# Attention ahead of two MoE layers: the 1e-9 of the softmax sums is added on ScalarE behind the last exponential, and the periodic order is placed anew

## The chip, the core and the metric

The kernel runs on one core of a Trainium2 chip. The core has TensorE (PE, matrix products and transposes), VectorE (DVE), ScalarE (ACT), GpSimd (POOL) and SyncE (SP, which issues the DMAs here). Each has its own queue and does its instructions in order; semaphores hold an instruction until what it reads or overwrites is ready. The metric is the device time of one execution in microseconds.

## The reference

Attention over 4 batches, 12 heads, 448 positions and 64 dimensions, with RMS-normalized q and k; its result goes, as 1792 rows of 768, through two MoE-like layers.

```python
q_n, k_n = (rmsnorm(q, g_q), rmsnorm(k, g_k))
scores = scale * np.matmul(q_n, k_n.transpose(0, 1, 3, 2))
scores = scores - np.max(scores, axis=-1, keepdims=True)
attn = np.exp(scores)
attn = attn / (np.sum(attn, axis=-1, keepdims=True) + 1e-09)
x = np.matmul(attn, v)                   # then to (batch * seq, heads * dim)
h = x @ moe_w_in;   x = (h / (1 + np.exp(-h))) @ moe_w_out
h = x @ moe2_w_in;  out = np.maximum(h, 0) ** 2 @ moe2_w_out
```

## The kernel before

**Attention** goes by pairs of heads: 4 batches of 6 pairs, 24 pairs. `prepare` loads q and k (qk), squares them, sums the squares (ms), makes the inverse root with a logarithm, an exponential and Newton steps (L641, L645, L649 to L664), multiplies (n, L672), transposes on TensorE (L684) and splits the result into an upper and a lower part (T; q_hi on ScalarE at L693 and L695, q_lo on VectorE at L700 and L702). `weigh` takes the 448 rows in three blocks of 128 for both heads and one block that mixes the last 64 rows of both (Q, Em). For each block TensorE makes the scores (L750, L757), VectorE the negated row maximum (mx, L772), ScalarE the exponential (E, L780), which also writes the sum of each row into one of the 7 columns of the tile `sum`. TensorE transposes E (L793), and ScalarE and VectorE copy the result from PSUM to SBUF (PTa and PTb, L563 and L565).

`attend` inverts the sums: on VectorE an add of 1e-9 (L823) and a reciprocal (L824), both in place on 128 x 7; TensorE transposes them (L820), VectorE copies them out (inv, L833), and SP stores them to DRAM and reads them back spread over the partitions (rd, R, L840 and L848). TensorE multiplies with v (L859), ScalarE copies that (xf), and GpSimd multiplies it by R (L879). The result is stored to DRAM (keep_x); of the first two batches it is also split into an upper part on ScalarE (x_hi, L575) and a lower part on GpSimd (x_lo, L584). Squares, Newton steps, the product n and Q run on GpSimd too, but for the first pairs.

**The MoE layers** follow on all 1792 rows, with every weight split into an upper and a lower part by ScalarE, VectorE and GpSimd.

**What sets the order.** A planner in the kernel (`Plan`) issues the steps. For attention it follows a table: step kind n of pair i stands at PERIOD x i plus its entry in LOADS or TABLE, plus a correction in FIRST for the first eight pairs; `plan.fix` ties a step to that place and to one engine. These numbers only sort the steps; on the chip each engine runs its queue as the semaphores allow. Steps without a place, all of the MoE layers among them, are put in by the planner by its own costs, and so move when the table moves.

The add and the reciprocal before, and their places:

```python
        def invert(e):
            nc.vector.tensor_scalar(sums.ap, sums.ap, 1e-9, None, ALU.add)
            nc.vector.reciprocal(sums.ap, sums.ap)
        step("invert", at, {"dve": (0.33, None, False)}, invert, writes=keys)
```

Of the kernel before, what the change touches and what calls it, by code (L numbers as in the profile page):

```python
# [9 lines left out]
F32 = mybir.dt.float32  # L10
# [3 lines left out]
AF = mybir.ActivationFunctionType  # L14
# [3 lines left out]
P = 128  # L18
# [20 lines left out]
PERIOD = 8.685  # L39
# [7 lines left out]
    "load_g": [1.36], "gains": [9.92], "warm": [-40.0],  # L47
    "load_qk": [-28.94, -23.71],
    "load_v": [1.94],
    "store_r": [22.9],  # L50
    "spread": [32.29, 33.29, 32.79],
    "keep_x": [54.22],
}
TABLE = {
    "squares": [-21.02, -18.06],
    "sums": [-7.69, -7.64],
    "log": [-3.92],
    "root": [-3.53],
    "newton": [-3.8, -2.59, -2.29, -1.99, -0.73],
    "norm": [1.57, 0.55],  # L60
    "turn_q": [6.83, 5.67],
    "q_hi": [8.48, 6.66],
    "q_lo": [9.18, 7.52],
    "scores": [13.72, 12.32, 13.07],
    "row_max": [15.15, 17.35, 13.28, 14.08, 14.62, 15.69, 16.81],
    "exp": [16.55, 18.85, 13.99, 14.74, 15.93, 17.6, 18.23],
    "turn_e": [19.76, 20.0, 19.13, 19.52, 20.23, 20.78, 20.47],
    "e_copy": [20.45, 20.59, 19.97, 19.97, 21.23, 21.23, 20.93, 22.3],
    "mask": [11.37],
    "mixed": [14.9],  # L70
    "attend": [24.63, 26.52],
    "invert": [19.61],
    "turn_s": [20.71],
    "inverse": [22.51],
    "pv_copy": [28.18],
    "attended": [38.49],
    "x_hi": [47.8],
    "x_lo": [74.71],
}
# [337 lines left out]
def kernel(  # L417
# [136 lines left out]

# [255 lines left out]
    def attend(i, vr, PT, sums, last):  # L810
# [938 lines left out]
```

## Time and profile before

| | us |
|---|---|
| median of 3 runs (lowest, highest) | 1142.46 (1142.25, 1143.43) |
| the profiled execution, its own time | 1144.96 |
| its span, first to last instruction | 1143.1 |
| busy in the span: PE, DVE | 1113.3, 945.9 |
| busy in the span: ACT, POOL | 609.4, 284.3 |

The span is cut into stretches below: two inside attention, its end, and the MoE layers. A share of busy time over the whole span says little, since TensorE fills the MoE layers and VectorE is the fullest engine of attention; the rows by stretch, the chain of work that ended last, and the timelines of single engines have to be read together. A matmul's row can be longer than the distance to the next one, since matmuls are pipelined; the same holds in a small way for ScalarE and VectorE. "Granted clock" is TensorE's, 1.00 for 2.4 GHz.

### The profile page before, as it was taken

How to read it: one execution, taken by the hardware profiler on the slowest of the kernel's cores; microseconds unless marked ns; L12 is line 12 of the kernel's file. 1: busy time of each engine (PE TensorE's matmuls, PEld its weight loads, DVE VectorE, ACT ScalarE, POOL GpSimd, SP SyncE). 2: the span in 40 equal slices, each digit the busy share in tenths (PEclk: the TensorE clock that was granted, in tenths of full speed). 3: DMA queues.
4: the chain of work that ended last, by engine and by line, in shares of the span. 5: the costliest groups of instructions: out<-in, count | busy, mean ns of one | idle time of the engine just before them, and what ended most of it. 6: DMA issues, size and time to landing. Idle time of an engine off the chain costs nothing.

```text
span 1143.1 us, 20235 instructions
## 1 busy us (share of the span) xinstructions
PE 1113.3 (97%) x7463; PEld 1000.7 (88%) x7463; DVE 945.9 (83%) x1660; ACT 609.4 (53%) x1273; POOL 284.3 (25%) x364
## 2 busy tenths in 40 slices
PE   8999999999999999999999999999999999999998
PEld 6776667779999898999999988999999999999997
DVE  7999999968687879887778798687888976888886
ACT  7988889965563547455554343544224435333321
POOL 5777788420101002100010010001230201122220
PEclk8999999999999999999999999999999999999999
DMA  7343344258646566677677579878758794555454
GB/s 185 99 123 121 109 122 125 84 177 275 210 148 219 161 207 216 224 251 250 221 264 228 196 232 360 290 277 318 276 194 300 239 330 180 180 192 181 168 171 132
DMA packets 122435, 235.29 MB, mean 206 GB/s; under 512 B 12216, under 2 KB 86112, under 8 KB 122336
## 3 DMA queue, kind: packets, MB, share of 16 engines
q1 hardware_dynamic: 122096, 233.80, 61.2%
q8 instruction: 59, 0.97, 0.3%
q14 instruction: 40, 0.33, 0.1%
q10 hardware_dynamic: 240, 0.20, 0.1%
HBM read 157.58 MB, written 76.37 MB: 205 GB/s over the span
## 4 chain that ended last, share of the span: by engine, by line
PE 72%; DVE 19%; ACT 5%; issue 2%; DMA 1%; POOL 0%; DVEq 0%; POOLq 0%; ACTq 0%
PE bank L1167 28%; PE bank L1265 18%; PE bank L1508 11%; PE bank L1632 7%; DVE mx L772 3%; PE bank L1078 3%; PE bank L859 2%; DVE sum L823 2%; ACT E L780 2%; DVE w L584 2%; PE bank L750 2%; DVE g L1182 2%; DVE PTa L565 1%; DVE gg L1527 1%; DVE ms L623 1%
## 5 line engine op out<-in xcount | busy, mean ns | idle before, releaser
L1265 PE MATMUL bank<-gg,w 128*128 128x448 f32 (+1 forms) x1168 | 239.9, 363 | 1.0 <-DVE gg L584 0.5
L1265 PEld LDWEIGHTS bank<-gg,w 128*128 128x128 f32 x1168 | 216.6, 188 | 19.4 <-DVE gg L584 1.1
L1182 DVE TENSOR_TENSOR g<-bank,g 128x448 f32<-128x448 f32 x180 | 108.6, 618 | 65.2 <-PE bank L1167 60.6
L1508 PE MATMUL bank<-w,gh 128*128 128x384 f32 (+1 forms) x564 | 144.3, 337 | 1.2 <-DVE gh L577 0.9
L1527 DVE TENSOR_TENSOR gg<-bank,gg 128x384 f32<-128x384 f32 (+1 forms) x197 | 103.5, 548 | 22.5 <-PE bank L1508 22.3
L1167 PE MATMUL bank<-yb,w 128*128 128x448 f32 (+1 forms) x548 | 119.0, 365 | 1.8 <-DVE w L584 1.6
L1167 PE MATMUL bank<-xb,w 128*128 128x448 f32 x528 | 115.8, 364 | 1.0 <-ACT g L563 0.7
L584 DVE TENSOR_TENSOR w<-W,w 128x768 fp32r<-128x768 f32 (+1 forms) x124 | 109.8, 892 | 7.4 <-ACT w L575 6.6
L1167 PEld LDWEIGHTS bank<-yb,w 128*128 128x128 f32 x548 | 100.8, 188 | 12.0 <-DVE w L584 4.1
L575 ACT CAST w<-W 128x768 fp32r<-128x768 f32 (+1 forms) x79 | 58.9, 747 | 93.1 <-DVE W L1143 25.6
L1167 PEld LDWEIGHTS bank<-xb,w 128*128 128x128 f32 x528 | 97.9, 188 | 9.5 <-ACT g L563 1.0
L1508 PEld LDWEIGHTS bank<-w,gh 128*128 128x128 f32 x564 | 102.7, 190 | 3.1 <-DVE gh L577 1.3
L1508 PE MATMUL bank<-w,gl 128*128 128x384 f32 (+1 forms) x282 | 95.2, 337 | 2.4 <-DVE gl L584 2.3
L780 ACT ACTIVATE E<-bank,mx 128x448 f32<-128x448 f32 x144 | 92.8, 651 | 5.0 <-DVE mx L772 4.1
L772 DVE TENSOR_REDUCE mx<-bank 128x1 f32<-128x448 f32 x168 | 94.6, 606 | 0.5 <-PE bank L750 0.5
L1433 ACT ACTIVATE g<-g 128x448 f32<-128x448 f32 x48 | 27.7, 578 | 121.8 <-DVE g L1182 121.3
L584 POOL TENSOR_TENSOR gl<-g,gh 128x448 fp32r<-128x448 f32 (+1 forms) x22 | 24.3, 1105 | 206.6 <-ACT gh L575 68.4
L1167 PE MATMUL bank<-xc,w 128*128 128x448 f32 x270 | 60.0, 366 | 0.0
L981 ACT ACTIVATE raw<-raw 128x768 int32<-128x768 uint16 (+1 forms) x72 | 59.3, 823 | 0.0
L750 PE MATMUL bank<-T 64*128 64x448 f32 x432 | 57.3, 382 | 1.1 <-ACT T L695 1.1
L1508 PEld LDWEIGHTS bank<-w,gl 128*128 128x128 f32 x282 | 53.5, 190 | 3.6 <-DVE gl L584 3.3
L1167 PEld LDWEIGHTS bank<-xc,w 128*128 128x128 f32 x270 | 50.7, 188 | 4.4
(179 smaller groups left out, 2217.3 us busy)
## 6 DMA issues: line engine op xcount, KB each, us to landing
raw<-in_moe_w_in_dram SPq DMA_DIRECT2D x32, 768.0 KB, 5.4
raw<-in_moe_w_out_dram SPq DMA_DIRECT2D x24, 512.0 KB, 4.1
raw<-in_moe_w_out_dram SPq DMA_DIRECT2D x16, 768.0 KB, 6.1
su<-w SPq DMA_DIRECT2D x16, 768.0 KB, 7.5
w<-su SPq DMA_DIRECT2D x16, 768.0 KB, 7.5
xf<-y SPq DMA_DIRECT2D x48, 224.0 KB, 4.9
xf<-x SPq DMA_DIRECT2D x39, 224.0 KB, 5.2
ki<-W SPq DMA_DIRECT2D x16, 384.0 KB, 5.3
```

Source lines behind the costliest of these rows:

```text
L575: nc.scalar.copy(o(), a())
L584: kind, when, any_t(n, rate), lambda e: engine(e).tensor_tensor(o(), a(), h(), ALU.subtract),
L750: nc.tensor.matmul(pts[j].ap[:, :S], T.ap[r, 0, a, c * CQ:(c + 1) * CQ], T.ap[r, 1, b_], start=(k_ == 0), stop=(k_ == 2),)
L772: lambda e, pt=pt, mx=mx: nc.vector.tensor_reduce(mx.ap, pt.ap[:, :S], AX.X, ALU.max, negate=True),
L780: lambda e, j=j, n=n, pt=pt, mx=mx, E=E: nc.scalar.activation(E.ap[:, j], pt.ap[:, :S], AF.Exp, bias=mx.ap, accum_out=sums.ap[:, n:n + 1]),
L981: lambda e: nc.scalar.activation(lo(), raw.ap[:, :2 * m].bitcast(U16).rearrange("p (m t) -> p m t", t=4)[:, :, 1], AF.Copy, bias=2.0 ** -1 ...
L1167: nc.tensor.matmul(pt.ap[:, c1:c2], w_()[:, c0 + c, :], view(b, a, c)()[:, c1:c2], start=(start and c == 0 and k == 0), stop=(c == HC - 1 ...
L1182: lambda e: nc.vector.tensor_tensor(o.ap, pt.ap[:, :S], a.ap, ALU.add),
L1265: nc.tensor.matmul(pt.ap[:, c1:c2], w_()[:, f, :], gg.ap[:, k, a, f, c1:c2], start=(f == 0 and n == 0), stop=(f == HQ - 1 and n == 2), ski ...
L1508: nc.tensor.matmul(pt.ap[:, :en], g.ap[:, fi, c0:c0 + P], w_()[:, 0, e0:e0 + en], start=(n == 0), stop=(n == 5),)
L1527: "acc", at, dve_t(n), lambda e: nc.vector.tensor_tensor(o(), pt.ap[:, :n], o(), ALU.add),
L1632: nc.tensor.matmul(pt.ap[:, :NH], a[i][0](m), b[j][0](), start=(start and k == 0), stop=(k == 2), skip_group_check=True,)
```

## The change

The tile `least`, one column of 1e-9, is set by GpSimd at the start. A new step "guard" on ScalarE adds it to the sums, by an Identity activation with `least` as its bias; "invert" is the reciprocal alone. PERIOD goes from 8.685 to 8.555, and all entries of LOADS, TABLE and FIRST are new.

```diff
-PERIOD = 8.685
+PERIOD = 8.555
...
-    "load_v": [1.94],
...
+    "load_v": [15.41],
...
-    "invert": [19.61],
...
-    "attended": [38.49],
-    "x_hi": [47.8],
-    "x_lo": [74.71],
...
+    "guard": [20.37],
+    "invert": [20.86],
...
+    "attended": [46.25],
+    "x_hi": [64.4],
+    "x_lo": [66.26],
...
+    least = sb([P, 1], F32, "least", 1)
+    step("ident", NOW, {"pool": (0.1, None, True)}, lambda e: nc.gpsimd.memset(least.ap, 1e-9), writes=[least])
...
-        def invert(e):
-            nc.vector.tensor_scalar(sums.ap, sums.ap, 1e-9, None, ALU.add)
-            nc.vector.reciprocal(sums.ap, sums.ap)
-
-        step("invert", at, {"dve": (0.33, None, False)}, invert, writes=keys)
+        step(
+            "guard", at, {"act": (0.13, None, False)},
+            lambda e: nc.scalar.activation(sums.ap, sums.ap, AF.Identity, bias=least.ap), reads=[least], writes=keys,
+        )
+        plan.fix(i, "guard")
+        step("invert", at, {"dve": (0.14, None, False)}, lambda e: nc.vector.reciprocal(sums.ap, sums.ap), writes=keys)
```

How the queues stand, in one pair from the middle of attention. VectorE before, from the sums of squares to the copies of the inverse sums:

```order
L623 TENSOR_REDUCE ms<-sq 112x16
L823 TENSOR_SCALAR sum<-sum 128x7
L824 RECIPROCAL sum<-sum 128x7
L565 COPY PTa<-bank_1938 112x8x64
L565 COPY PTa<-bank_1966 112x8x64
L565 COPY PTb<-bank_1989 112x8x64
L772 TENSOR_REDUCE mx<-bank_2022 128x1
L833 COPY inv<-bank_2000 7x64
```

VectorE with the change:

```order
L626 TENSOR_REDUCE ms<-sq 112x16
L568 COPY PTa<-bank_1934 112x8x64
L568 COPY PTa<-bank_1954 112x8x64
L830 RECIPROCAL sum<-sum 128x7
L568 COPY PTb<-bank_1976 112x8x64
L775 TENSOR_REDUCE mx<-bank_2010 128x1
L837 COPY inv<-bank_1998 7x64
```

The add is gone from VectorE, and the reciprocal stands behind both PTa copies.

ScalarE before, from the copy of the product with v to the next pair's first exponential:

```order
L563 COPY xf<-bank_2722 128x448
L563 COPY PTa<-bank_2762 112x8x64
L563 COPY PTa<-bank_2791 112x8x64
L563 COPY PTb<-bank_2825 112x4x64
L563 COPY PTb<-bank_2813 112x8x64
L575 CAST xb<-xf 128x448
L641 ACTIVATE y<-ms,tiny 112x16
L563 COPY PTb<-bank_2826 112x4x64
L645 ACTIVATE y<-y 112x16
L780 ACTIVATE E,sum<-bank_2847,mx 128x448
```

ScalarE with the change:

```order
L566 COPY xf<-bank_2510 128x448
L566 COPY PTa<-bank_2550 112x8x64
L827 ACTIVATE sum<-sum,least 128x7
L566 COPY PTa<-bank_2572 112x8x64
L566 COPY PTb<-bank_2616 112x4x64
L566 COPY PTb<-bank_2594 112x8x64
L566 COPY PTb<-bank_2615 112x4x64
L644 ACTIVATE y<-ms,tiny 112x16
L578 CAST xc<-xf 128x448
L783 ACTIVATE E,sum<-bank_2628,mx 128x448
```

The guard (L827) stands between the two PTa copies; two of the PTb copies (112x4x64) read the bank into which TensorE also transposes the sums.

TensorE before, around the transposes of the sums (L820):

```order
L793 MATMUL bank_2620<-ident,Em 112x64
L820 MATMUL bank_2619<-ident,sum 7x64
L820 MATMUL bank_2620<-ident,sum 7x64
L793 MATMUL bank_2607<-ident,E 112x64
L793 MATMUL bank_2608<-ident,E 112x64
```

TensorE with the change, where the transposes of the sums are L823:

```order
L753 MATMUL bank_2628<-T 128x448
L753 MATMUL bank_2629<-T 128x448
L823 MATMUL bank_2615<-ident,sum 7x64
L823 MATMUL bank_2616<-ident,sum 7x64
L753 MATMUL bank_2644<-T 128x448
```

The transposes of the sums now stand behind the first six score products of the next pair, where before they stood right behind the transposes of Em.

## Rows read from the trace of the kernel before

**Rows 1.** Busy us (and count) of each engine by stretch, granted clock, DMA, GB/s.
```profile
75.64:167.47 91.83, 83.49 (x1071) 62.35 (x1071) 88.50 (x153) 78.20 (x226) 71.83 (x110) 1.00 0.38 115
167.47:239.36 71.89, 71.15 (x975) 55.61 (x975) 69.44 (x134) 67.64 (x191) 44.04 (x69) 1.00 0.34 103
239.36:247.54 8.18, 6.16 (x50) 3.77 (x46) 5.78 (x11) 3.02 (x6) 1.25 (x2) 0.79 0.64 201
247.54:1143.10 895.56, 882.86 (x4555) 823.14 (x4553) 715.96 (x1237) 396.18 (x673) 118.18 (x95) 1.00 0.67 229
```

**Rows 2.** The chain that ended last: start us, us, what; through L823.
```profile
75.64 1.66 DVE sum L823
...
116.48 1.61 DVE sum L823
...
126.67 1.62 DVE sum L823
...
167.47 0.91 DVE sum L823
...
203.56 0.71 DVE sum L823
...
212.47 0.71 DVE sum L823
```

**Rows 3.** By line: durations ns min/median/max, first and last start us.
```profile
L823 DVE TENSOR_SCALAR sum<-sum x24: 171/891/1650, 20.9 to 239.4; 128x7 f32<-128x7 f32 x24
...
L824 DVE RECIPROCAL sum<-sum x24: 200/201/204, 21.6 to 240.5; 128x7 f32<-128x7 f32 x24
```

**Rows 4.** VectorE's timeline: start us, us, engine, line, instruction.
```profile
203.49 0.77 DVE L823 TENSOR_SCALAR sum<-sum 128x7 f32<-128x7 f32 x1
204.29 0.20 DVE L824 RECIPROCAL sum<-sum 128x7 f32<-128x7 f32 x1
```

**Rows 5.** GpSimd's timeline at the same two places.
```profile
116.34 0.61 POOL L734 TENSOR_TENSOR Q<-T,half 128x256 fp32r<-128x256 f32 x1
116.92 1.13 POOL L879 TENSOR_TENSOR xf<-xf,R 128x448 f32<-128x448 f32 x1
...
203.09 1.14 POOL L879 TENSOR_TENSOR xf<-xf,R 128x448 f32<-128x448 f32 x1
204.31 0.20 POOL L649 TENSOR_SCALAR nwm<-ms 112x16 f32<-112x16 f32 x1
```

**Rows 6.** ScalarE's timeline; in brackets the idle time before, and its releaser.
```profile
118.62 0.86 ACT L563 COPY PTb<-bank 112x256 f32<-112x256 f32 x2 [0.78 <-PE bank L820]
...
120.88 0.37 ACT L563 COPY PTb<-bank 112x256 f32<-112x256 f32 x1 [0.73 <-DVE inv L833]
...
205.55 0.32 ACT L641 ACTIVATE y<-ms,tiny 112x16 f32<-112x16 f32 x1
205.76 0.37 ACT L563 COPY PTb<-bank 112x256 f32<-112x256 f32 x1
...
206.81 0.63 ACT L780 ACTIVATE E<-bank,mx 128x448 f32<-128x448 f32 x1 [0.56 <-DVE mx L772]
```

**Rows 7.** TensorE's timeline: the shortest pair, and the end of attention.
```profile
31.46 0.22 PE L820 MATMUL bank<-ident,sum 64*7 64x64 f32 x2
...
35.27 1.95 PE L859 MATMUL bank<-PTa,vv 112*64 112x256 f32 x16
...
39.91 0.22 PE L820 MATMUL bank<-ident,sum 64*7 64x64 f32 x2
...
240.75 0.22 PE L820 MATMUL bank<-ident,sum 64*7 64x64 f32 x2 [1.30 <-DVE sum L824]
...
242.87 3.44 PE L859 MATMUL bank<-PTa,vv 112*64 112x256 f32 x16
```

**Rows 8.** Waits of TensorE from 232 us on: us in total, times, longest.
```profile
PE bank L1508 <- DVE gl L584: 2.3, 2, 1.9
```

**Rows 9.** DMA issues from 60 to 180 us: count, KB each, us to landing.
```profile
vv<-in_v_dram SPq DMA_DIRECT2D x12, 224.0 KB, 2.8
```

More of the change, by code (lines that the diff above doesn't have):

```diff
@@ L58 @@
[L58 to L69, printed above, removed]
@@ L70 @@
-    "mixed": [14.9],
-    "attend": [24.63, 26.52],
-    "invert": [19.61],
-    "turn_s": [20.71],
-    "inverse": [22.51],
-    "pv_copy": [28.18],
-    "attended": [38.49],
-    "x_hi": [47.8],
-    "x_lo": [74.71],
+    "squares": [-16.41, -14.39],
+    "sums": [-7.56, -7.51],
+    "log": [-3.79],
+    "root": [-2.57],
+    "newton": [-4.71, -2.31, -2.01, -1.71, -1.41],
+    "norm": [-0.07, 1.95],
+    "turn_q": [5.55, 6.08],
+    "q_hi": [6.78, 7.2],
+    "q_lo": [7.4, 8.46],
+    "scores": [13.48, 11.91, 12.73],
@@ new lines @@
+    2: {"load_qk": [13.67, 11.81], "squares": [6.7, 5.04], "sums": [2.96, 2.96], "load_v": [-4.52], "log": [0.44], "root": [0.42], "newton": [1.36, 0.42, 0.42, 0.42, 0.41], "norm": [-0.62, -0.62], "q_hi": [-0.16, -0.15], "q_lo": [0.08, 0.09], "scores": [-0.05, -0.05, -0.05], "exp": [-0.25, -0.25, -0.3, -0.25, -0.25, -0.25, -0.25], "turn_e": [-0.05, -0.05, -0.05, -0.05, -0.05, -0.05, -0.05], "e_copy": [-0.25, -0.05, -0.25, -0.05, -0.25, -0.05, -0.25, -0.25], "mask": [-2.45], "mixed": [-0.05], "attend": [-0.11, -0.11], "guard": [-0.25], "invert": [-0.05], "turn_s": [-0.1], "inverse": [-0.05], "pv_copy": [-0.3], "store_r": [-1.93], "spread": [-1.26, -1.49, -1.62], "attended": [-0.66], "keep_x": [1.49], "x_hi": [0.25], "x_lo": [0.88]},
@@ new lines @@
+    3: {"load_qk": [6.02, 4.16], "squares": [2.54, 1.05], "sums": [0.43, 0.43], "load_v": [-4.59], "log": [0.04], "root": [-0.17], "newton": [-0.5, -0.17, -0.17, -0.17, -0.17], "norm": [-1.21, -1.21], "q_hi": [-0.22, -0.22], "scores": [-0.07, -0.07, -0.07], "exp": [-0.27, -0.27, -0.33, -0.27, -0.27, -0.27, -0.27], "turn_e": [-0.07, -0.08, -0.07, -0.07, -0.07, -0.07, -0.07], "e_copy": [-0.27, -0.07, -0.27, -0.07, -0.27, -0.07, -0.27, -0.27], "mask": [-2.5], "mixed": [-0.07], "attend": [-0.12, -0.12], "guard": [-0.27], "invert": [-0.07], "turn_s": [-0.12], "inverse": [-0.07], "pv_copy": [-0.33], "store_r": [-1.74], "spread": [-1.27, -1.52, -1.64], "attended": [0.46], "keep_x": [1.53], "x_hi": [0.29], "x_lo": [0.92]},
@@ new lines @@
+    4: {"load_qk": [5.38, 3.52], "squares": [-0.38, -0.38], "sums": [0.12, 0.12], "load_v": [-1.73], "log": [-0.09], "root": [-0.23], "newton": [-1.08, -0.23, -0.23, -0.23, -0.23], "norm": [-1.27, -1.27], "turn_q": [-0.04, -0.04], "q_hi": [-0.24, -0.23], "scores": [-0.09, -0.09, -0.09], "row_max": [-0.04, -0.04, -0.04, -0.05, -0.04, -0.05, -0.04], "exp": [-0.29, -0.29, -0.34, -0.29, -0.3, -0.3, -0.3], "turn_e": [-0.09, -0.09, -0.09, -0.09, -0.09, -0.09, -0.09], "e_copy": [-0.29, -0.09, -0.29, -0.09, -0.29, -0.09, -0.29, -0.29], "mask": [-1.32], "mixed": [-0.09], "attend": [-0.15, -0.15], "guard": [-0.29], "invert": [-0.09], "turn_s": [-0.14], "inverse": [-0.09], "pv_copy": [-0.34], "store_r": [-1.76], "spread": [-1.3, -1.08, -1.2], "attended": [0.5], "keep_x": [1.56], "x_hi": [0.32], "x_lo": [0.95]},
@@ new lines @@
+    5: {"load_qk": [-1.66, -3.07], "squares": [-0.96, -0.96], "sums": [0.06, 0.06], "load_v": [-1.76], "log": [-0.14], "root": [-0.25], "newton": [-1.14, -0.25, -0.25, -0.25, -0.25], "norm": [-1.29, -1.29], "turn_q": [-0.06, -0.06], "q_hi": [-0.26, -0.26], "scores": [-0.11, -0.11, -0.11], "row_max": [-0.06, -0.07, -0.06, -0.06, -0.06, -0.06, -0.06], "exp": [-0.31, -0.31, -0.37, -0.31, -0.31, -0.31, -0.31], "turn_e": [-0.11, -0.12, -0.11, -0.11, -0.11, -0.11, -0.11], "e_copy": [-0.31, -0.12, -0.31, -0.11, -0.31, -0.11, -0.31, -0.31], "mask": [-1.34], "mixed": [-0.11], "attend": [-0.17, -0.16], "guard": [-0.31], "invert": [-0.11], "turn_s": [-0.17], "inverse": [-0.11], "pv_copy": [-0.31], "store_r": [-1.33], "spread": [-0.17, 0.04, -0.08], "attended": [0.54], "keep_x": [1.6], "x_hi": [0.36], "x_lo": [0.99]},
```

35 lines of the change are left out of this document (19 added, 16 removed).

## The prediction

> **What bounds the kernel now.** I read four views in this order: busy time by stretch, the chain that ended last in the attention part, the instructions of the line that the change takes off VectorE, and the timelines of the engines next to it.
>
> The program has two parts. From 247.54 us to the end the two MoE layers run; TensorE is busy 882.86 of those 895.56 us [rows 1]. The 24 head pairs of attention lie before that. In them VectorE is the fullest engine: 88.50 of 91.83 us from 75.64 to 167.47, 69.44 of 71.89 us after that [rows 1]. So in attention it is VectorE's own queue that is worth shortening, and the MoE layers gain only what starts earlier.
>
> The chain shows what in that queue is odd. It runs through the add on the sums at L823, which touches 7 columns: from 116.48 to 126.67 us, one pair, the add alone is 1.61 us of the chain, and in the calmer stretch from 203.56 to 212.47 it is 0.71 us [rows 2]. By line, the add took 171 ns at least, 891 in the median and 1650 at most, over 24 pairs, while the reciprocal of the same 7 columns right behind it took 200 to 204 ns every time [rows 3]. So the length is a wait inside the add, not work. GpSimd's timeline says for what: the add that starts at 203.49 lasts 0.77 us, to 204.26, and the multiply by the inverse sums on GpSimd (L879) runs from 203.09 to 204.23; the add of 116.48 lasts to 118.09, and L879 runs from 116.92 to 118.05 [rows 2, 4, 5]. The add ends 0.03 and 0.04 us behind GpSimd's instruction. In the second case it began while the one ahead of L879 (L734, 116.34 to 116.95) was on GpSimd, and stood through both. In the stretch with the long waits, 75.64 to 167.47, a pair takes 10.20 us (91.83 us for nine), and GpSimd is busy 71.83 us of it, since it also splits the first two batches there [rows 1, 2]. From the first add to the last it is 218.5 us for 23 intervals, 9.50 in the mean [rows 3], so 126.7 us for the other 14, 9.05 each.
>
> **What the change removes.** The add goes to ScalarE as an activation with a bias (the "guard"), right behind the first of ScalarE's PTa copies; VectorE keeps the reciprocal, now behind two PTa copies of its own. VectorE's period without the add: 8.91 from add to add at 203.56 less 0.71 is 8.20 us [rows 2]. The reciprocal did not lengthen, although GpSimd ran beside it: L649 starts at 204.31 and takes its usual 0.20, inside the reciprocal's 204.29 to 204.49 [rows 4, 5]. So I cost the lost wait at its full length.
> For this the Trainium skill has a rule, "SBUF — State Buffer", section "Who interferes with whom": copy, cast and tensor_scalar on VectorE can enter a mode that needs the port pair shared with GpSimd, and the one that comes second blocks for the whole instruction; the reciprocal is not in that list. The trace agrees for the tensor_scalar add (0.03 and 0.04 us behind GpSimd's end); for a reciprocal that comes in the middle of a long GpSimd instruction no row here shows it.
>
> **What it adds.** One ScalarE instruction a pair, 128x7. No row shows it; the nearest is the logarithm, also a few columns with a bias from memory: it is followed by the next copy 0.21 us after its start (205.55 to 205.76) [rows 6]. I take 0.21; the ends are 0, where ScalarE would have waited anyway, and 0.32, the logarithm's whole length [rows 6]. The guard waits for sums that ScalarE itself made, with two copies between. The reciprocal now waits for the guard, and behind it in VectorE's queue stand its PTb copy and the next pair's first row maximum, for which ScalarE's next exponential waits; ScalarE has four copies and a logarithm of its own to do until then, which hide it, and the first rival prices it without that cover. The memset of the new constant on GpSimd is in the startup, once, and hidden by the loads.
> One page speaks against the move: "ScalarE: Activation LUTs", section "Rules for kernel authors", says to add on VectorE, not ScalarE, and budgets about 0.3 us for an activation with such a bias. By 0.3 instead of 0.21 the twelve tightest pairs below would cost 1.1 us more, and the estimate would be 1123.4 instead of 1122.3.
>
> **What then bounds a pair.** Every engine is close, so I take each in turn. ScalarE, in a pair with the extra split copy x_hi: 10.20 less its two waits of 0.78 and 0.73 is 8.69, with the guard 8.90; without x_hi: 8.91 less 0.56 is 8.35, with the guard 8.56 [rows 2, 6]. These are upper values, since a wait is counted from the end of the instruction ahead, and the next can start 0.1 to 0.2 before that end (the logarithm, above); so 8.6 to 8.9 and 8.4 to 8.56. TensorE did all its work of a pair in 8.45 once (31.46 to 39.91) [rows 7]; the new order puts six score products between the transposes of Em and of the sums, two more changes of kind, up to 0.3. GpSimd, with x_lo: 71.83 us for nine pairs, 8.0 each [rows 1]. VectorE 8.20. I take 8.8 for the twelve pairs with x_hi and 8.55 for the other eleven intervals: 12 x 8.8 + 11 x 8.55 = 199.65, that is 18.9 us under 218.5. The ends are the engines' own lowest sums (8.6 and 8.4: 195.6, a gain of 22.9) and 0.3 more in each (9.1 and 8.9: about 207.1, a gain of 11.4).
>
> **What is moved.** x_hi, the stores of x (keep_x) and the multiply L879 come some 8 to 17 us later behind their pair than before, x_lo 8 us earlier, the load of v 13.5 us later, with a lead of about 9 us over its use against 2.8 us to land [rows 9]. On SP's queue the late L879 means that a store of x or a spread waits longer in it, with the loads of q and k behind; by the table those are issued some 12 us ahead of the squares that read them, so this costs nothing unless the queue is held some 8 us. The split of x is needed only by the MoE layers, and all of it is done before they begin. At the end of attention VectorE has weight work ahead of the last add, and TensorE waits 1.30 us there [rows 7]; in the new order that work stands behind the reciprocal, beside the 3.2 us of the last attend. I count 1.3 us for that, from 0 (the first weights then come late by as much) to 2.6 (the low clock of that place goes too).
> **MoE layers.** The same matmuls; the small work is shared out anew (17 instructions fewer on VectorE, 13 more on ScalarE, 4 more on GpSimd). TensorE is idle 12.7 of 895.56 us there [rows 1], and the largest reason, a split on VectorE, makes 2.3 us [rows 8]. I cost it at 0; the ends, -3 and +4, are about the size of that reason, once and twice.
>
> **Sum.** 18.9 + 1.3 = 20.2 us. The profiled span of 1143.1 becomes 1122.9; that run's own time was 1144.96, 1.86 over its span, so 1124.8 in such a run. The median of the three runs, 1142.46, is 2.50 under the profiled run; from it **1122.3 us**. All low ends together: 28.5 us, 1114.0. All high ends: 11.4 - 4 = 7.4 us, 1135.1.
>
> **Rivals.**
> *The wait moves to ScalarE.* Its PTb copies wait for the transposed sums, which now need guard, reciprocal and, on TensorE, six score products first. For it: both of ScalarE's waits in rows 6 are at exactly this place. Against: those waits were made by the add (1.61 us), which is gone. If half of one, 0.4 us, stays in every pair: 23 x 0.4 = 9.2, so 1131.5.
> *The reciprocal takes over the wait for GpSimd,* the change not doing what it says. Then only the add's own 0.17 goes, 23 x 0.17 = 3.9: 1138.5. For it: in rows 3 it never came while a long GpSimd instruction was already running. Against: L649 beside it, above.
> *TensorE's clock falls in attention.* The one way that I see to a slower kernel. The granted clock was 0.79 from 239.36 to 247.54, between the levels 1.2 and 2.4 GHz, behind TensorE's wait of 1.30 us, and the attend there took 3.44 against 1.95 us, 1.76 times [rows 1, 7]. At the low level a pair is 8.45 x 1.76 = 14.9 on TensorE, 6.2 more than forecast, so from four such pairs on the gain is gone; six give 1159.5. Against: the clock was 1.00 from 75.64 to 167.47, where TensorE was idle 8.3 of 91.83 us [rows 1], more than it will be now.
>
> **How the numbers follow.** Forecast 0.73, the wait on ScalarE 0.17, the reciprocal's wait 0.06, the low clock 0.04. The range 1114 to 1135 holds nearly all of the first two. About 0.2% (2.3 us) is what a measurement of this kernel can tell from no change. Both likely cases lie beyond that; of the reciprocal's case half falls within it. Faster 0.93, same 0.03, slower 0.04.
>
> **What would show it.** Right: reciprocals of 0.20 us wherever GpSimd is; no chain from 75 to 167 us through VectorE's sum; the last transpose of sums near 220 us instead of 240.75; pairs of 8.5 to 8.9 us; MoE layers still near 895 us. Wrong: reciprocals of 0.7 us and more; ScalarE waiting 0.4 us or more a pair for L823's transposes; a granted clock under 0.95 between 75 and 220 us; MoE layers changed by more than 4 us.

## The result, and the profile with the change

The changed kernel takes 1125.97 us (median of 4 runs, 1125.59 to 1127.55) where the kernel before took 1142.95 beside it: a ratio of 0.9854, interval 0.9837 to 0.9871, 17.0 us less. The forecast was 1122.3, with a range of 1114 to 1135. Its profiled execution has a span of 1124.2 us, 18.9 under the 1143.1 of before; that run's own time was 1125.93.

By stretch (windows; the columns are span of the stretch, then busy time and instructions of PE, PEld, DVE, ACT, POOL, then granted clock, DMA share, GB/s):

```profile
20.00:72.72 52.72, 52.58 (x753) 41.36 (x753) 51.07 (x101) 52.50 (x159) 39.84 (x66) 1.00 0.46 132
72.72:176.93 104.21, 103.86 (x1430) 79.91 (x1428) 99.23 (x193) 104.20 (x313) 95.95 (x146) 1.00 0.47 137
176.93:218.50 41.57, 41.17 (x583) 32.01 (x580) 36.34 (x76) 41.34 (x120) 21.07 (x34) 1.00 0.31 89
218.50:226.00 7.50, 6.22 (x48) 4.72 (x49) 5.24 (x7) 4.78 (x8) 1.41 (x1) 1.00 0.39 105
226.00:1124.20 898.20, 880.73 (x4544) 823.29 (x4543) 708.01 (x1222) 401.51 (x683) 124.90 (x98) 1.00 0.67 230
```

In the second row, the pairs with the split x_hi, ScalarE is busy 104.20 of 104.21 us: it has taken VectorE's place as the full engine (in rows 1, VectorE had 88.50 of 91.83), with TensorE close to it at 103.86. TensorE's clock is 1.00 in every row, also at the end of attention, where it was 0.79 [rows 1]. The last row is a mean over 898 us, in which two short places of a lowered clock do not show; they are taken up with e10.

The two small instructions by line (the last numbers are busy us, mean ns of one, idle us ahead), VectorE's and ScalarE's:

```profile
L830 DVE RECIPROCAL sum<-sum 128x7 f32<-128x7 f32 x24 | 4.6, 191 | 0.0
L827 ACT ACTIVATE sum<-sum,least 128x7 f32<-128x7 f32 x24 | 9.0, 376 | 0.0
```

The add of rows 3 took 891 ns in the median; nothing of that kind is left. How a reciprocal stands to GpSimd is seen in the timelines, first VectorE's, then GpSimd's (start us, us):

```profile
115.23 0.68 DVE L568 COPY PTa<-bank 112x512 f32<-112x512 f32 x1
115.83 0.19 DVE L830 RECIPROCAL sum<-sum 128x7 f32<-128x7 f32 x1
115.94 0.64 DVE L568 COPY PTb<-bank 112x512 f32<-112x512 f32 x1
...
115.15 1.05 POOL L613 TENSOR_TENSOR sq<-qk 112x512 f32<-112x512 f32 x1
```

It starts 0.68 us into a GpSimd instruction of 1.05 us and takes its 0.19. 19 of the 24 reciprocals overlap a GpSimd instruction; all 24 took 189 to 193 ns.

The transposes of sums (by source line) give the pairs: first at 21.9 us, last at 218.5, where rows 7 had the last at 240.75; the one wait for them on ScalarE is 0.3 us in all.

```profile
L823 PE MATMUL bank<-ident,sum x48: 213/214/220, 21.9 to 218.5; 64*7 64x64 f32 x48
...
  ACT PTb L566: 0.3, 1
```

From one to the next it is 8.67 us in most pairs with x_hi (10.20 before, rows 2) and 8.43 in most without (8.91 before).

The trace's difference adds up: first to last transposes 196.6 us for 218.5, a gain of 22.0; from the last transposes to the eleventh matmul of the MoE layers 6.7 for 7.9, a gain of 1.2; 0.3 before the first transposes; and from that eleventh matmul to the end 898.9 us for 894.4, a **loss of 4.5**. Together 19.0, which is the difference of the spans (18.9 is that of the rounded ones). Most of the loss comes early. TensorE's timeline (in brackets the wait and its releaser) and, below it, SP's queue with the loads of weights:

```profile
286.54 0.47 PE L1171 MATMUL bank<-yb,w 128*128 128x448 f32 x1 [0.59 <-ACT w L578]
287.54 3.94 PE L1171 MATMUL bank<-yb,w 128*128 128x448 f32 x17 [0.52 <-DVE w L587]
301.33 2.51 PE L1171 MATMUL bank<-xb,w 128*128 128x448 f32 x9 [2.51 <-ACT g L566]
...
266.54 0.38 SPq L973 DMA_DIRECT2D raw<-in_moe_w_in_dram  x1
272.62 0.38 SPq L973 DMA_DIRECT2D raw<-in_moe_w_in_dram  x1
275.74 0.38 SPq L973 DMA_DIRECT2D raw<-in_moe_w_in_dram  x1
284.46 0.38 SPq L973 DMA_DIRECT2D raw<-in_moe_w_in_dram  x1
```

Counted in matmuls, TensorE loses 6.5 us on the kernel before between its matmuls 300 and 400 of the MoE layers (284 to 308 us), with these three waits and a granted clock of 0.93 from 284 to 310 us, where the kernel before had no wait and 1.00. Later places take and give 1 to 2 us each.

### The profile page after: what moved, and what is told of

Read it like the earlier page. It is cut to its first block, busy times and chain, and to the rows that moved or that the text cites. A ratio compares the mean times of both kernels' runs of the same rounds, so it can differ in the third digit from the quotient of the medians.

```text
span 1124.2 us, 20358 instructions
## 1 busy us (share of the span) xinstructions
PE 1099.9 (98%) x7463; PEld 994.6 (88%) x7463; DVE 912.9 (81%) x1619; ACT 617.2 (55%) x1310; POOL 291.7 (26%) x369
## 4 chain that ended last, share of the span: by engine, by line
PE 56%; DVE 6%; ACT 1%; issue 1%; DMA 0%; DVEq 0%; ACTq 0%
PE bank L1171 26%; PE bank L1269 13%; PE bank L1512 11%; PE bank L1636 7%; DVE w L587 1%; DVE g L1186 1%; DVE gg L1531 1%; DVE gg L1688 0%; ACT g L1437 0%; ACT g L1443 0%; DVE gl L587 0%; DVE W L1128 0%; DMA y<-g 0%; DVE W L1147 0%; DVE w L580 0%
## 5 line engine op out<-in xcount | busy, mean ns | idle before, releaser
L587 DVE TENSOR_TENSOR w<-W,w 128x768 fp32r<-128x768 f32 (+1 forms) x124 | 112.6, 915 | 5.3 <-ACT w L578 4.2
L578 ACT CAST w<-W 128x768 fp32r<-128x768 f32 (+1 forms) x82 | 61.5, 750 | 77.9 <-PE bank L1269 21.1
L587 POOL TENSOR_TENSOR gg<-g,gg 128x448 fp32r<-128x448 f32 x11 | 14.8, 1347 | 169.5 <-ACT gg L578 97.3
L587 POOL TENSOR_TENSOR gl<-g,gh 128x448 fp32r<-128x448 f32 (+1 forms) x18 | 18.9, 1052 | 150.9 <-ACT gh L578 82.3
```

Source lines behind the costliest of these rows:

```text
L578: nc.scalar.copy(o(), a())
L587: kind, when, any_t(n, rate), lambda e: engine(e).tensor_tensor(o(), a(), h(), ALU.subtract),
```

## The experiments

Four questions were open: did the add's wait make the pairs long, or the order; what is the guard's price, and what would come cheaper; what bounds a pair now; and what took the 4.5 us in the MoE layers. In e1 to e4, e7 and e8 the planned times were left alone, so that each queue keeps the order of the kernel it comes from, but for what the edit says; e5, e6 and e9 to e11 move the starts of steps. Times by part, in us, from the traces, each of which is one run, up to 2.5 us from its kernel's median (before 2.5 over, e1 2.3 under): "attention" is first to last transposes of sums, "MoE" is the eleventh matmul of the MoE layers to the end. The ratio is to the kernel before on the same chip, with its 95% interval.

| kernel | the 1e-9 | attention | MoE | span | ratio |
|---|---|---|---|---|---|
| before | VectorE, old order | 218.5 | 894.4 | 1143.1 | 1 |
| e1 | ScalarE, old order | 201.1 | 891.7 | 1121.4 | 0.9855 [0.9837, 0.9874] |
| e2 | VectorE, new order | 202.7 | 902.1 | 1133.3 | 0.9929 [0.9912, 0.9946] |
| changed | ScalarE, new order | 196.6 | 898.9 | 1124.2 | 0.9854 [0.9837, 0.9871] |
| e3 | left out | 194.7 | 900.9 | 1123.6 | 0.9860 [0.9834, 0.9885] |
| e4 | behind the transposes | 206.6 | 901.0 | 1137.0 | 0.9959 [0.9947, 0.9972] |
| e5 | ScalarE, MoE in old order | 197.8 | 892.6 | 1117.9 | 0.9810 [0.9795, 0.9824] |
| e6 | ScalarE, stores of x early | 196.6 | 899.1 | 1123.0 | 0.9871 [0.9851, 0.9890] |
| e7 | VectorE, two tensors | 202.7 | 897.7 | 1129.1 | 0.9921 [0.9903, 0.9939] |
| e8 | ScalarE, twice | 203.6 | 900.4 | 1132.4 | 0.9926 [0.9911, 0.9941] |
| e9 | weight work ahead | 196.6 | 899.0 | 1122.7 | one run |
| e10 | one copy ahead | 196.4 | 900.4 | 1124.9 | one run |
| e11 | both | 196.6 | 897.3 | 1120.8 | one run |

### The add alone, and the order alone

In the kernel before, the guard is issued with the exponential that is a pair's last:

```diff
-                    lambda e, j=j, n=n, pt=pt, mx=mx, E=E: nc.scalar.activation(
-                        E.ap[:, j], pt.ap[:, :S], AF.Exp, bias=mx.ap, accum_out=sums.ap[:, n:n + 1]),
+                    lambda e, c=c, j=j, n=n, pt=pt, mx=mx, E=E: [nc.scalar.activation(
+                        E.ap[:, j], pt.ap[:, :S], AF.Exp, bias=mx.ap, accum_out=sums.ap[:, n:n + 1])] + ([
+                        nc.scalar.activation(sums.ap, sums.ap, AF.Identity, bias=least.ap)] if (c, j) == (0, 1) else []),
...
-            nc.vector.tensor_scalar(sums.ap, sums.ap, 1e-9, None, ALU.add)
             nc.vector.reciprocal(sums.ap, sums.ap)
```

> The kernel before with its own order on every engine; only the add moves: ScalarE adds the 1e-9 right behind the pair's last exponential, VectorE keeps the reciprocal at its old place. Theory A (the add's wait for GpSimd made the pairs long): a pair loses the wait, 0.9 us in the median and up to 1.5, until ScalarE with the guard is full (8.6 to 8.9); from the first transposes of sums to the last it takes 203 to 208 us where the kernel before took 218.5, and the span ends 10 to 16 us earlier. Rival B (the gain of the change is the new order; the add alone was one of several late things on VectorE): 213 us or more, a gain under 6 us.

Attention took 201.1 us, even a little less than theory A's 203 to 208; 17.4 of the 22.0 us come with the add alone. The pairs with x_hi became 8.89 us, the others 8.52. By line, and its chain of waits (start us, us):

```profile
L782 ACT ACTIVATE sum<-sum,least 128x7 f32<-128x7 f32 x24 | 7.3, 302 | 0.8
L824 DVE RECIPROCAL sum<-sum 128x7 f32<-128x7 f32 x24 | 4.8, 201 | 10.0 <-ACT sum L782 10.0
...
117.49 0.62 ACT E L780 x2
118.11 0.02 issue
118.14 0.04 ACT sum L782
118.18 0.17 issue
118.34 0.51 ACT xf L563
118.85 0.97 ACT PTa L563 x2
```

Of the 38 pieces of the chain between 110 and 130 us, a few of "issue" apart, all are ScalarE's; VectorE can wait 10.0 us for the guard, and it costs nothing. In the chain of before, VectorE's sum stood there with 1.61 us a pair [rows 2].

In the changed kernel, the add goes back (the steps "guard" and "invert"):

```diff
-            lambda e: nc.scalar.activation(sums.ap, sums.ap, AF.Identity, bias=least.ap), reads=[least], writes=keys,
+            lambda e: None, reads=[least], writes=keys,
...
-  lambda e: nc.vector.reciprocal(sums.ap, sums.ap)
+  lambda e: [nc.vector.tensor_scalar(sums.ap, sums.ap, 1e-9, None, ALU.add), nc.vector.reciprocal(sums.ap, sums.ap)]
```

> The changed kernel with its order unchanged; only the add goes back to VectorE, just ahead of the reciprocal, and the guard on ScalarE goes. Theory A: the adds last from 0.17 to about 1.6 us again, most end within 0.1 us of a GpSimd instruction's end, and a pair of the first two batches takes 9.2 us and more; first to last transposes of sums 205 to 215 us against 196.6 of the changed kernel, 8 to 18 us longer. Rival B: the new order has so much room on VectorE that the wait hides; under 3 us longer.

The wait is back, but attention is 202.7, between the two theories: 6.1 us longer than in the changed kernel, with pairs of 8.50 to 9.55 us (the last 7.80). By line, first in the kernel before and then in e2, and on e2's timelines of VectorE and GpSimd:

```profile
L823 DVE TENSOR_SCALAR sum<-sum 128x7 f32<-128x7 f32 x24 | 25.6, 1069 | 2.7 <-ACT E L780 2.1
...
L830 DVE TENSOR_SCALAR sum<-sum 128x7 f32<-128x7 f32 x24 | 10.2, 426 | 0.0
...
110.51 0.30 DVE L830 TENSOR_SCALAR sum<-sum 128x7 f32<-128x7 f32 x1
110.84 0.20 DVE L830 RECIPROCAL sum<-sum 128x7 f32<-128x7 f32 x1
...
109.73 1.04 POOL L613 TENSOR_TENSOR sq<-qk 112x512 f32<-112x512 f32 x1
```

The add starts 0.78 us into GpSimd's 1.04 and so waits only for the rest. Of the 24 adds the longest is 1.19 us and the median 0.35. Less its own 0.158 (the shortest), the adds waited 6.4 us in all, which is the 6.1 that attention lost. In the old order they waited 21.5 us (25.6 us for 24, less 24 times the 0.171 of [rows 3]), since they began early in a GpSimd instruction or stood through two. So the two halves of the change overlap: the move of the add alone gives 17.4 us, the new order alone 15.8, both 22.0. Theory A's mechanism is shown; that it is worth its full length whatever the order is not.

### What the guard costs, and what else there was

> The changed kernel in its own order with the 1e-9 left out altogether: no guard, the reciprocal of the bare sums. It prices the guard. If ScalarE sets the pairs of 8.67 us and TensorE those of 8.43: the first fall to 8.45 to 8.50, the others stay, 2.3 us less over the attention part. If ScalarE sets both: 0.2 less in each, 4.6 us. If TensorE or the chain through the transposes sets both: no change (under 0.5 us). In each case the MoE layers stay as they are in the changed kernel, since every queue keeps its order.

Here the edit is the first half of e2's, without its second. Attention was 194.7, 1.9 less: 8.45 to 8.48 us for 8.67 in six of the pairs with x_hi, 8.41 for 8.43 in those without. Four later pairs with x_hi stayed at 8.65 to 8.69. TensorE is busy 33.98 of 34.00 us there, but also 33.95 of 34.00 where the pairs fell, so this does not tell why; that stays open. So the first case, ScalarE in the pairs with x_hi, holds for most of them. That TensorE, with 8.41 us, is right behind it in both kinds is argued from these lengths. The guard costs 0.2 us in a pair where it costs, as priced from the logarithm [rows 6].

```diff
-            lambda e: nc.scalar.activation(sums.ap, sums.ap, AF.Identity, bias=least.ap), reads=[least], writes=keys,
+            lambda e: [nc.scalar.activation(sums.ap, sums.ap, AF.Identity, bias=least.ap) for _ in range(2)], reads=[least], writes=keys,
```

> The changed kernel in its own order with the guard issued twice (1e-9 added twice). Without the guard the pairs of 8.67 us fell to 8.47 and those of 8.43 to 8.41. If ScalarE is full in the first only, and TensorE sets the second: 8.87 and 8.43 to 8.5, about 2.5 us more in attention. If ScalarE has just become full in both: 8.87 and 8.63, 4.6 us more. If the chain through reciprocal and transposes counts as well, more than 4.6.

7.1 us more, the third case by its number: nearly every pair is 0.31 us longer (8.98 and 8.75). ScalarE's timeline, the two guards as one row:

```profile
117.79 0.68 ACT L566 COPY PTa<-bank 112x512 f32<-112x512 f32 x1
118.27 0.74 ACT L827 ACTIVATE sum<-sum,least 128x7 f32<-128x7 f32 x2
118.91 0.56 ACT L566 COPY PTa<-bank 112x512 f32<-112x512 f32 x1
```

From the first guard to the next copy it is now 0.64 us where the single one had 0.21. As I read it, one guard overlaps with the copies beside it, and the second has to wait for the first, whose result it adds to. So the price of a small ScalarE instruction depends on its neighbours, and more work on ScalarE now lengthens both kinds of pair. The Trainium skill, "ScalarE: Activation LUTs", "Rules for kernel authors", budgets about 0.3 us for such an activation: its length in e1 was 0.302, but what it took from the queue was 0.2.

Next, the guard's step and "invert" issue nothing, and the step "inverse" does both:

```diff
             for h, pe in enumerate(last):
-                nc.vector.tensor_copy(inv.ap[:, h * D:(h + 1) * D], pe.ap[:NS, 2 * CQ:2 * CQ + D])
+                nc.vector.tensor_scalar(inv.ap[:, h * D:(h + 1) * D], pe.ap[:NS, 2 * CQ:2 * CQ + D], 1e-9, None, ALU.add)
+            nc.vector.reciprocal(inv.ap, inv.ap)
```

> The changed kernel in its own order, but the bare sums are transposed, VectorE's two copies of them out of PSUM become the add of 1e-9 (128 columns in two, read from PSUM), and one reciprocal of 7x128 stands behind; guard and old reciprocal go. ScalarE loses the guard, as in the kernel without one: 2.3 us less if that is ScalarE's price. Theory A with the ports: an add that reads PSUM lasts as long as the copies do now (under 0.2 us) wherever GpSimd is, and VectorE has room for the reciprocal: 2 to 3 us less than the changed kernel. Rival: this add too waits for GpSimd (0.7 us and more), or the longer reciprocal fills VectorE: as the changed kernel or up to 8 us longer.

Half of the expectation held, that of the add from PSUM; the kernel was 10 us longer than the changed one in attention. By line:

```profile
L837 DVE TENSOR_SCALAR inv<-bank 7x64 f32<-7x64 f32 x48 | 8.3, 206 | 0.3 <-ACT PTb L566 0.3
L838 DVE RECIPROCAL inv<-inv 7x128 f32<-7x128 f32 x24 | 22.6, 941 | 0.8
```

An add with a constant that reads PSUM never waits for GpSimd (201 to 213 ns, 48 times). But the reciprocal takes 941 ns for 128 columns against 191 for 7, so 750 ns for 121 more columns, an estimate of 6.2 ns each, while the add and the copy of 64 columns take 0.2 us with all that goes with them. It filled VectorE, which was busy 103.75 of the 104.21 us from 72.72 to 176.93: nearly every pair became about 9.05 us.

Then e2 with another form of the add:

```diff
-  nc.vector.tensor_scalar(sums.ap, sums.ap, 1e-9, None, ALU.add)
+  nc.vector.tensor_tensor(sums.ap, sums.ap, least.ap.to_broadcast([P, 7]), ALU.add)
```

> The changed kernel in its own order; the guard goes and VectorE adds the 1e-9 again, but as a sum of two tensors (the sums and the column of 1e-9 repeated over 7 columns) instead of a tensor with a constant. If the wait belongs to the form of the instruction (the Trainium skill, SBUF, lists copy, cast and tensor_scalar, not a sum of two 32-bit tensors): the adds last 0.15 to 0.2 us wherever GpSimd is, attention 194.5 to 196.5, as without a guard. If every SBUF to SBUF add waits: 0.16 to 1.2 us, ending some 0.03 us behind GpSimd, attention 202 to 203 as with the first form put back.

It waits as the first form did:

```profile
L830 DVE TENSOR_TENSOR sum<-sum,least 128x7 f32<-128x7 f32 x24 | 9.8, 408 | 0.0
...
84.02 0.98 DVE L830 TENSOR_TENSOR sum<-sum,least 128x7 f32<-128x7 f32 x1
...
83.93 1.04 POOL L613 TENSOR_TENSOR sq<-qk 112x512 f32<-112x512 f32 x1
```

It starts 0.09 us behind GpSimd's L613 and ends at 85.00, with GpSimd's end at 84.97. My expectation gave the rule of the Trainium skill only in half: the same section of "SBUF — State Buffer", "Who interferes with whom", goes on that an instruction of VectorE with two inputs in SBUF contends with a GpSimd instruction that reads SBUF, and that one with a single input outside the two-port modes does not. With that, it agrees with every run here: tensor and constant, and two tensors, wait (e2, e7); the reciprocal (one input in SBUF) and the add from PSUM do not.

### The 4.5 us of the MoE layers

In the changed kernel the plan is made twice, with the tables of before (start0, at0) and with its own; then all steps are issued in the order of their starts, each behind what it needs:

```diff
+        for s in steps:
+            if s.nom is None and s.when[0] in ("seg", "end"):
+                start[s.n], at[s.n] = start0[s.n] - shift, at0[s.n]
```

> Attention in the changed kernel's order, MoE layers in the order of the kernel before: the plan is made with both tables; attention steps keep the places of the changed kernel, all other steps the engine and the time that the plan of before gives them, shifted by the difference between the two ends of attention. The stores of x stay at the changed kernel's late places. Theory O (the MoE layers of the changed kernel lost 4.5 us, of these 6.4 between its matmuls 300 and 400, to the order that the planner gave their small work): the 6.4 are gone, first to last transposes of sums 196.6 as in the changed kernel, MoE layers 891.5 to 894.5, span 1117 to 1120. Theory D (they were lost to the transfers that the shorter attention pushes together at its end): 5 us or more of the loss stay, span 1123 and more.

Theory O. The MoE layers take 892.6 us, TensorE stands within 0.02 us of the kernel before from matmul 10 to matmul 700, and the span is 1117.9. Attention was 197.8, since the last pair is 1.2 us longer, and the way from there to the MoE layers 1.3 shorter. It is the fastest kernel of the study: 1119.74 us (median of 4 runs), its interval apart from the changed kernel's. Its loads of weights (SP's queue), with TensorE's MoE work beginning within 0.05 us of where the changed kernel's does:

```profile
262.67 0.38 SPq L1061 DMA_DIRECT2D raw<-in_moe_w_in_dram  x1
267.32 0.38 SPq L1061 DMA_DIRECT2D raw<-in_moe_w_in_dram  x1
274.54 0.38 SPq L1061 DMA_DIRECT2D raw<-in_moe_w_in_dram  x1
280.61 0.38 SPq L1061 DMA_DIRECT2D raw<-in_moe_w_in_dram  x1
```

They are 3.9, 5.3, 1.2 and 3.9 us earlier than in the changed kernel. The plan of before places the loads and the small work of the MoE layers together, so e5 does not part the two.

For the other theory, the changed kernel's plan stays, and ahead of issuing only the stores' places are moved:

```diff
+        for s in self.steps:
+            if s.kind == "keep_x":
+                start[s.n] -= 10.42
```

> The changed kernel with one thing moved: each store of x (keep_x) stands 10.42 us of plan time earlier in SP's queue, where the kernel before had it; the other queues keep their order to the instruction. Theory D: the transfers that pile up behind attention (16 DMA engines full from 232.7 to 242.7 us) thin out, the weight loads of 262 to 285 us come 3 to 5 us earlier, and 3 to 6.4 us of the loss in the MoE layers go: span 1118 to 1121. Theory O: weights may come earlier, but the 6.4 us stay (under 1 us gained), since ScalarE's and VectorE's copies of TensorE's results stand ahead of the weight work in their queues. Both: attention within 1 us of 196.6.

Theory D falls. From 225 to 245 us the DMA engines went from a share of 1.00 to 0.88 (windows of e6 here, its MoE work 1.3 us earlier than the changed kernel's), the four loads of weights came at the same times of the MoE work as in the changed kernel, and the waits stayed to the hundredth:

```profile
225.00:245.00 20.00, 20.00 (x106) 18.64 (x105) 11.59 (x19) 13.14 (x21) 1.16 (x1) 1.00 0.88 302
...
285.24 0.47 PE L1187 MATMUL bank<-yb,w 128*128 128x448 f32 x1 [0.59 <-ACT w L594]
286.23 3.94 PE L1187 MATMUL bank<-yb,w 128*128 128x448 f32 x17 [0.52 <-DVE w L603]
300.02 3.30 PE L1187 MATMUL bank<-xb,w 128*128 128x448 f32 x9 [2.51 <-ACT g L582]
```

The last three kernels looked for the single places. In each the plan's start of a few steps, named by number, is moved before they are issued, as in e6. In e9 these are pieces of the work on four weight tiles:

```diff
+SOONER = {1853: 1.5, 1864: 0.6, 1865: 0.6, 1866: 1.6, 1877: 3.2, 1878: 3.2, 1879: 3.2, 1882: 2.4, 1883: 2.4, 1884: 2.4}
...
+            start[s.n] -= SOONER.get(s.n, 0.0)
```

> The changed kernel with ten instructions moved by one to four places in their queues, all of them work on four weight tiles between 262 and 285 us (ScalarE's L980 and L985, VectorE's L992): each now stands ahead of a copy of a TensorE result (L1288, L1290 or L568) that it stood behind. All other places, SP's queue too, stay. Theory Q (a weight tile's work waits behind a copy that waits for TensorE, so the next load, for which its buffer must be free, starts late, and this adds up over four loads): the loads of weights issued at 272.62, 275.74 and 284.46 us come 1 to 3 us earlier, and of the 6.4 us lost between matmuls 300 and 400 at least 1.9 are back at matmul 350. Rival: the weight work was late by its own chain of loads, and the copies only seem to hold it: under 0.5 us back.

The theory fell: counted from the beginning of the MoE work, the loads moved by 0.4, 0.1, -0.2 and 2.2 us, and at matmuls 350 and 400 nothing was back. The copies ahead of the weight work only seemed to hold it; what held it stays open. In e10 it is the copy, and the two pieces of weight work ahead of it:

```diff
+SOONER = {1947: 1.6, 1974: -1.0, 1944: -1.0}
```

> The changed kernel with one instruction moved by two places: ScalarE's copy L566 for which TensorE waits 2.51 us at 301.33 now stands ahead of two pieces of weight work (L985 and L578) instead of behind them. If that order made the wait: it falls by 0.8 to 1.4 us, with the stretch of low clock behind it perhaps another 2. If TensorE's result itself was late: under 0.3 us.

For the wait, this one held. TensorE's timeline:

```profile
299.19 2.09 PE L1189 MATMUL bank<-xb,w 128*128 128x448 f32 x9 [1.14 <-ACT g L584]
...
302.36 1.89 PE L1189 MATMUL bank<-yb,w 128*128 128x448 f32 x8 [0.87 <-DVE w L605]
```

The wait of 2.51 us became 1.14, with a new one of 0.87 behind it; 1.8 us were back at matmul 400. By matmul 1000 the kernel had lost 1.6 of that again, and its MoE part ended at 900.4.

Most of both is TensorE's clock. Below are windows of 10 us around this wait: of the changed kernel, of e10, and of e7, whose MoE layers have the changed kernel's order, with that copy where it was. Then come e10's next place of a lowered clock (0.83 is a mean over both levels, 1.2 and 2.4 GHz) and e7's wait:

```profile
300.00:310.00 10.00, 8.67 (x36) 7.90 (x37) 7.96 (x13) 5.19 (x10) 1.15 (x1) 0.83 0.30 88
...
300.00:310.00 10.00, 9.13 (x48) 8.18 (x47) 8.77 (x14) 5.07 (x10) 1.19 (x1) 1.00 0.49 150
...
306.20:316.20 10.00, 8.70 (x44) 8.03 (x45) 9.39 (x14) 5.22 (x11) 1.39 (x1) 1.00 0.44 125
...
410.00:420.00 10.00, 8.09 (x33) 7.05 (x32) 8.60 (x15) 6.43 (x12) 1.49 (x1) 0.83 0.32 100
...
307.50 2.13 PE L1171 MATMUL bank<-xb,w 128*128 128x448 f32 x9 [2.51 <-ACT g L566]
```

e7 has the full wait of 2.51 us, and yet it has lost 5.0 us at matmul 400 where the changed kernel has lost 6.5: its clock did not fall behind the wait. So 1.5 of e10's 1.8 us come without the move too, and only about 0.3 is shown for the copy's place. Whether the shorter wait keeps the clock up is not shown: behind the wait of 2.51 us the clock fell in seven kernels of eight.

The last kernel has both:

```diff
+SOONER = {1853: 1.5, 1864: 0.6, 1865: 0.6, 1866: 1.6, 1877: 3.2, 1878: 3.2, 1879: 3.2, 1882: 2.4, 1883: 2.4, 1884: 2.4, 1947: 1.6, 1974: -1.0, 1944: -1.0}
```

> Both moves, of e9_weights_first and of e10_copy_first. Theory Q for both: nearly all of the 6.4 us is back at matmul 400, and the span falls from 1124 to 1118 to 1120 us. If later places in the MoE layers take back what is gained here, the gain at matmul 400 is there and the span stays above 1122.

1.7 us at matmul 400, as e10, kept to the end: 897.3 us, with one place of lowered clock in the MoE layers (0.83 from 684 to 694 us). But e7, with neither move, also has one (0.83 from 690 to 700) and 897.7, so the gain cannot be put down to the two moves. That the 6.5 us lie in the order of loads and small work, with the clock that fell behind the waits, is shown by e5 and e6; which places make them, and why the loads come late in that order, stays open.

The clock also tells why kernels of one order differ. In the changed kernel's MoE order the layers take 897.3 and 897.7 us with one such place (e11, e7), 898.9 to 899.1 with two (changed, e9, e6), 900.4 to 900.9 with three (e8, e10, e3) and 902.1 with four (e2); e4, which had lost 0.7 us by matmul 50, is left out. In the old order they take 891.7 and 892.6 with none (e1, e5) and 894.4 with one (before, 0.89 from 900 to 915 us). One place costs about 1.5 us, by e7 beside the changed kernel at matmul 400. As an estimate from these, the loss of 4.5 us is 1.5 for one place more and 3.0 for the order, and e1's 2.7 under before is 1.5 for one place less, with 1.2 open.

## Why the prediction was right, and where not

**What bounds the kernel.** Right: VectorE's queue with the add in it. ScalarE's waits in attention, 20.8 us in before by its table of waits (8.6 and 8.1 for the inverse sums, 4.1 for row maxima), are gone in the changed kernel, whose table has none from 20 to 218 us. The rows of before:

```profile
ACT PTb L563 <- DVE inv L833: 8.6, 12, 0.7
ACT PTb L563 <- PE bank L820: 8.1, 11, 0.8
ACT E L780 <- DVE mx L772: 4.1, 7, 0.7
```

**The add costs its wait's full length.** Shown by e1 and e2 as a mechanism. But the step put the whole gain on it, in any order; e2 shows that the new order alone takes 15.1 of the 21.5 us of waiting away.

**The guard, 0.21 us.** Right: 0.20 by e3, and not 0.3.

**A pair, 8.8 and 8.55.** They measured 8.67 and 8.43, both near the low ends of 8.6 and 8.4. The term was mis-sized: 12 times 8.8 and 11 times 8.55 counted ScalarE's waits from the end of the instruction ahead, which I had named as an upper value, and then took the value near the upper end; and the 0.3 us for TensorE's two changes of kind did not appear, as the pairs of 8.41 us in e3 speak for. First to last came out at 196.6 where the sum had 199.65: 3.1 us more gain.

**The end of attention, 1.3.** It measured 1.2, and the low clock is gone.

**The MoE layers, 0, from -3 to +4.** The step that failed: 4.5 us longer, half a microsecond beyond the end. I had counted how few instructions change engines and took the size of the largest single wait for the bound. But the new table also moved the loads and the order of ScalarE's and VectorE's small work there, and that costs by its places and not by its counts; e5 gives it back. Nor did the term hold anything for the clock: about 1.5 of the 4.5 us is one place of lowered clock more than before, behind such waits. This is what lies between 1122.3 and 1125.97: 4.5 us lost here and 3.1 more won in the pairs make, with smaller terms, 1.3 in the span (1124.2 for 1122.9). The other 2.4 is no work: the profiled run of before lay 2.5 us over its median, and I carried that over; that of the changed kernel lies on its median. That the forecast came this near is in part luck, since its two misses, in the pairs and in the MoE layers, go opposite ways.

**The rivals.** The wait on ScalarE's PTb copies did not come (0.3 us in all); the reciprocal never waited; the clock stayed at 1.00 between 20 and 226 us. The cover that I named for VectorE's wait is shown in e1: 10.0 us of waiting for the guard at no cost.

## What to carry to other kernels

A tiny instruction with a long median and a short minimum is a wait: find whose end it shares, and move it to an engine or a form that has no part in that lock, before the order is touched. In this kernel the add's move alone, in the old order, was worth as much as the move with a whole new table (ratios 0.9855 and 0.9854), because what the table gained in attention was lost again in the layers behind, whose order was a by-product. So when a new table comes out of a planner, keep the parts that it was not made for in their old order and look at each part's time by itself. And before 1 or 2 us between two traces are put down to an edit, compare the granted clock of the same work in short windows: e10's gain was for the most part a clock that did not fall, as in e7 without the edit.

## What the runs showed of the hardware

- VectorE's add on SBUF can stand through two GpSimd instructions in a row: in ten pairs of before it began within the first and ended with the second, as at 116.48 us [rows 2, 5], and in e2 once (1.19 us). It need not: eight times in e2 it ended 0.03 us behind the first, with the next already following. What decides is not shown.
- A reciprocal took 191 ns for 128x7 and 941 for 7x128, five times as long, an estimate of 6.2 ns a column (the two differ in partitions too): the shape in which few columns stand beside many partitions was the cheap one.
- Two dependent ScalarE instructions of 7 columns cost 0.43 us more than the step of one, a pair 0.31 us; a lone one between copies costs 0.2.
- TensorE's mean granted clock differs from run to run of one kernel, and the time with it: e3 took 1122.92 us at a mean granted clock of 0.997 and 1127.40 at 0.992.
- The time ahead of the first transposes of sums was 20.3 us in e11 and 21.9 in the changed kernel, whose queues are the same until then. The granted clock from 10 to 22 us was 1.00 in e11 and 0.86 in the changed kernel, where 16 score products took 3.28 us for 1.91. A span compared with another to better than 2 us has to be compared part by part.
